# One soft-cap attention and soft mixture-of-experts kernel: two instead of three of every seven chunks share their exponential with VectorE, and the dispatch transposes and sums stand earlier in the loop

## The chip, the cores and the metric

The kernel runs on one core of a Trainium2 chip. The metric is the device time of one launch in microseconds (us). The kernel before the change took 330.87 us, the median of three runs that lie between 330.65 and 331.65 us.

In a core, TensorE multiplies matrices (PE in the profile; PEld is its loading of weights), ScalarE evaluates functions such as tanh and exp (ACT), VectorE does elementwise work (DVE), GpSimd does casts, copies and issues DMAs (POOL), and SyncE issues DMAs (SP). Each engine takes its own instructions in the order in which the program gives them, and an instruction that waits for another engine holds up all that stand behind it.

## The reference, cut to what matters

```python
# q, k, v: (8 batches, 12 heads, 448 tokens, 64); cap = 30
scores = (q @ k.T) / sqrt(64)
scores = cap * tanh(scores / cap)
attn   = softmax(scores, axis=-1)
x      = (attn @ v) as (8 * 448, 768)

# soft mixture of experts: phi (768, 32), w1 (8, 768, 1024), w2 (8, 1024, 768)
logits = x @ phi
d = softmax(logits, axis=0)                  # over all 3584 tokens: into the 32 slots
slot_in = d.T @ x                            # 4 slots for each of the 8 experts
slot_out[e] = relu(slot_in[e] @ w1[e]) @ w2[e]
c = softmax(logits, axis=1)                  # over the 32 slots: back to the tokens
out = c @ slot_out
```

## The kernel before, in words

**Attention.** Twelve heads of a batch are three quads of four heads, so there are 24 quads, each of two pairs of heads. The scores of a pair are 7 tiles of 128 keys (64 of either head) by 448 queries. The 336 tiles of all pairs are cut into 56 chunks of 6, and the main loop runs over chunks, `for j in range(NCH)`. Seven chunks are one batch, so the loop's pattern repeats with a period of seven iterations, and an iteration is named below by its number or by j % 7. In iteration j

- ScalarE does tanh on the two halves of chunk j (line 291, three tiles each, from PSUM) and then exp on the whole of chunk j - 1 (line 295), in place in the buffer `ex`. The scores are capped, so no maximum is taken off;
- TensorE multiplies `ex` of an earlier pair with v (line 331, `pv`, in two passes that share one PSUM buffer), and makes the scores of both halves of chunk j + 1 (line 282, `sc`, two PSUM buffers);
- VectorE normalizes each pass (lines 341 and 342, `rec` and `xq`).

**Work between.** Everything else is put into this loop by hand: `at(j, slot, f, ...)` hangs a call into a slot of iteration j. Slot "0" is at the iteration's start, "a" follows the first pass of `pv`, "b" the first half of the next scores, "c" the second pass of `pv`, and "d" the second half of the next scores. What shares a slot runs in the order in which it was hung there. Among these calls are the transposes of k and q (line 250, `kps` and `qps`, copied out by VectorE at 252 as `kT` and `qT`), the casts of v by GpSimd (260 and 261), transposes of x and logits (357 and 368, `xps` and `lps`, taken out at 359 and 373), matmuls on a tile of ones without a use of their own (`spare`, 521, `junk`), and DMAs of the weights by GpSimd (109 and 113).

For batch b with j = 7b there are also `e_exp` (line 379: the exponentials `E` of the logits, repeated fourfold by GpSimd at 385 as `e`) in iteration j + 11, `e_norm` (392 `zps`: their sum over tokens, added to `zacc` at 396, or copied there at 394 for batch 0) in j + 13, `e_transp` (404 `eps`: four transposes, copied out as `ET` at 405) and, for every other batch, `e_sums` (414 `wps`, and a reciprocal `winv` at 415). The transposes `kps`, `qps`, `xps`, `eps` and the results `lps`, `zps`, `wps` all use one PSUM buffer, `psT`: what comes next on TensorE waits until the engine that reads the one before has done so.

**The shared exponentials.** For a chunk j in the list `shared`, ScalarE's exp leaves the first of the six tiles out (it is `128x2240` in place of `128x2688`), and VectorE computes that tile in three parts of seven instructions on 128x448 elements: part 0 makes the exponent and the mantissa from bits (lines 307, 309, 311), part 1 and part 2 evaluate a polynomial (313, 314, then 316, 317). In the kernel before, `shared` holds the chunks with j % 7 of 1, 3 and 5 from 8 on, 20 in all.

**After the loop** come the last pairs, the slots' sums, the two layers of the experts (weights loaded to the chip or, for part of the second layer, to DRAM and from there once attention's buffers are free), and the output tiles, which VectorE and ScalarE take out and SyncE stores.

Of the kernel before, what the change touches and what calls it, by code (L numbers as in the profile page):

```python
# [32 lines left out]
def kernel(  # L33
# [20 lines left out]
    cap = float(cap)  # L54
# [6 lines left out]
    NCH = NTILE // CH  # L61
# [237 lines left out]

    shared = [j for j in range(NCH - 2) if j % 7 in (1, 3, 5) and j > 7] if cap < 80 else []

    def poly_exp(j, part):
        t, bits = exs[j][:, 0, :], 2.0 ** 23
# [135 lines left out]
    def at(j, slot, f, *a):  # L441
        if j < 0:
            j, slot = 0, "b"
        aux.setdefault((j, slot), []).append((f, a))
# [8 lines left out]
    def quad_in(Q, cast_k, cast_q, k_in, q_in, v_in):  # L453
        if 0 < Q < NQ:
            for nm, when in (("k", cast_k), ("q", cast_q)):
                at(*when, *((cast, nm) if Q == 1 else (load, nm, Q + 1)))
            at(*k_in, transp, "k", Q)
            at(*q_in, transp, "q", Q)
            at(*v_in, vcast, Q)

    for b in range(B):
        j = b * PER
        if b == 0:
            quad_in(1, (0, "a"), (0, "b"), (0, "d"), (1, "a"), (2, "d"))
        else:
            quad_in(3 * b + 1, (j - 1, "b"), (j, "a"), (j - 1, "d"), (j, "c"), (j + 1, "d"))
        quad_in(3 * b + 2, (j, "d"), (j + 1, "c"), (j + 2, "b"), (j + 2, "d"),
                (j + 4, "d"))
        quad_in(3 * b + 3, (j + 4, "a"), (j + 5, "a"), (j + 3, "d"), (j + 5, "c"),
                (j + 6, "d"))  # L470
        p = 6 * b
        at(j + 1, "d", spare, 34 if b == 0 else 10)
        at(j + 2, "d" if b == 0 else "a", spare, 4 if b == 0 else 14)
        if b:
            at(j + 2, "c", spare, 8)
        at(j + 3, "d", spare, 10 if b == 0 else 4)
        at(j + 4, "a", x_transp, p)
        at(j + 5, "a", x_transp, p + 1)
        at(j + 6, "a", x_transp, p + 2)
        at(j + 5, "d", logits, 3 * b)  # L480
        if b < B - 1:
            at(j + 7, "a", x_transp, p + 3)
            at(j + 8, "a", x_transp, p + 4)
            at(j + 7, "d", logits, 3 * b + 1)
            at(j + 9, "a", x_transp, p + 5)
            at(j + 9, "d", logits, 3 * b + 2)
            at(j + 11, "0", e_exp, b)
            at(j + 11, "d", slot_sums, b)
            if b < B - 2:
                at(j + 15, "c", e_transp, b)  # L490
            if b < B - 2:
                at(j + 13, "d", e_norm, b)
            if b % 2:
                at(j + 15, "d", e_sums, b // 2)
    for j in shared:
        for part, (dj, slot) in enumerate(((0, "a"), (0, "c"), (1, "b" if j % 7 == 1 else "a"))
                                          if j % 7 < 5 else ((0, "c"), (1, "a"), (1, "c"))):
            at(j + dj, slot, poly_exp, j, part)
    for n, job in enumerate(wjobs):
        at(1 + n * (NCH - 5) // len(wjobs), "b", *job)  # L500
    for j, slot, n in ((0, "a", 10), (0, "c", 10), (1, "b", 10), (1, "c", 8)):
# [251 lines left out]
    for n in range(B // 2 * NT):  # L753
        bb, c = divmod(n, NT)
# [61 lines left out]
```

## Time and profile before, and how to read it

| | before |
|---|---|
| median of three runs | 330.87 us |
| the profiled execution | 330.65 us, of which the span from the first to the last instruction is 328.9 us |
| busy: PE, ACT, DVE, POOL | 279.5, 278.6, 214.9, 141.3 us |
| mean granted TensorE clock | 0.95 of full speed |
| exp by ACT (line 295) | 132.1 us in 58 instructions: 35 of 128x2688, 20 of 128x2240, and 3 smaller at the end |
| tanh by ACT (line 291) | 141.3 us in 113 instructions |
| DMA moved on average | 206 GB/s |

A row of a timeline gives the start in us, the duration in us, the engine, the line, the operation, what it writes and reads with shapes, and how often; in square brackets stands the idle time of the engine just before, with what ended it. A row of the waits gives who waited for whom, and then the time in total, how often, and the longest. A row of the stages gives the window, its length, each engine's busy time with the number of instructions in brackets (PE, PEld, DVE, ACT, POOL), the granted clock of TensorE, the mean busy share of the DMA engines (overlapping packets can bring it above 1) and GB/s.

Iterations are found in the trace by ScalarE's rows: two tanh and one exp are one iteration. Iteration 9 starts at 47.38 us, 16 at 82.29, 23 at 116.60, 30 at 152.02, 37 at 185.98, 44 at 220.12 and 51 at 254.40 us. Tanh of the last chunk is done before 278.6 us.

### The profile page before, as it was taken

How to read it: one execution, taken by the hardware profiler on the slowest of the kernel's cores; microseconds unless marked ns; L12 is line 12 of the kernel's file. 1: busy time of each engine (PE TensorE's matmuls, PEld its weight loads, DVE VectorE, ACT ScalarE, POOL GpSimd, SP SyncE). 2: the span in 40 equal slices, each digit the busy share in tenths (PEclk: the TensorE clock that was granted, in tenths of full speed). 3: DMA queues.
4: the chain of work that ended last, by engine and by line, in shares of the span. 5: the costliest groups of instructions: out<-in, count | busy, mean ns of one | idle time of the engine just before them, and what ended most of it. 6: DMA issues, size and time to landing. Idle time of an engine off the chain costs nothing.

```text
span 328.9 us, 9405 instructions
## 1 busy us (share of the span) xinstructions
PE 279.5 (85%) x4071; PEld 195.9 (60%) x4071; DVE 214.9 (65%) x521; ACT 278.6 (85%) x208; POOL 141.3 (43%) x178
## 2 busy tenths in 40 slices
PE   8899989979997979979897899799979898998710
PEld 6667666656665656756575567576656667753300
DVE  3624577775788578767876767877786674427830
ACT  4999999996999799979998999989997999326720
POOL 4584660852566452575367516643761230000000
PEclk9999999987999799979997999999988999999975
DMA  7999999899799999999799997999899428977996
GB/s 258 205 198 180 223 189 220 158 180 226 137 156 190 232 168 155 163 196 195 126 184 221 176 189 129 185 230 205 141 205 195 107 96 259 343 267 290 390 411 250
DMA packets 57481, 67.64 MB, mean 206 GB/s; under 512 B 3808, under 2 KB 53600, under 8 KB 57440
## 3 DMA queue, kind: packets, MB, share of 16 engines
q0 software_dynamic: 42448, 35.31, 70.3%
q1 hardware_dynamic: 14704, 31.50, 27.7%
q8 instruction: 32, 0.52, 0.6%
q10 hardware_dynamic: 288, 0.23, 0.2%
q14 instruction: 9, 0.07, 0.1%
HBM read 91.32 MB, written 18.87 MB: 335 GB/s over the span
## 4 chain that ended last, share of the span: by engine, by line
PE 40%; DVE 33%; ACT 18%; DMA 3%; issue 2%; DVEq 0%; ACTq 0%
PE pv L331 14%; ACT ex L291 9%; ACT ex L295 8%; PE sc L282 7%; DVE xq L342 6%; DVE xp L314 3%; DVE ex L317 3%; PE junk L521 3%; PE xps L357 3%; PE kps L250 3%; DVE xp L316 2%; DVE xp L313 2%; DVE xm L309 2%; DVE rec L341 2%; DMA out_dram<-ob 2%; DVE xe L311 2%
## 5 line engine op out<-in xcount | busy, mean ns | idle before, releaser
L291 ACT ACTIVATE ex<-sc 128x1344 bf16<-128x1344 f32 (+1 forms) x113 | 141.3, 1317 | 15.0 <-PE pv L331 7.7
L295 ACT ACTIVATE ex<-ex 128x2688 bf16<-128x2688 bf16 (+4 forms) x58 | 132.1, 2282 | 0.1
L331 PEld LDWEIGHTS <-ex 128*128 128x128 bf16 x1344 | 81.7, 100 | 24.5 <-DVE xq L342 11.4
L331 PE MATMUL pv<-vbd,ex 128*128 128x130 bf16 x1274 | 93.2, 226 | 2.3 <-DVE xq L342 0.8
L282 PE MATMUL sc<-qT,kT 64*64 64x448 bf16 x672 | 80.1, 367 | 1.7 <-ACT ex L291 1.5
L260 POOL CAST vbd<-vraw 64x896 bf16<-64x896 f32 x23 | 23.1, 1006 | 69.5 <-PE pv L331 50.6
L341 DVE RECIPROCAL rec<-pv 128x4 f32<-128x4 f32 x91 | 16.5, 181 | 38.8 <-PE pv L331 38.8
L342 DVE TENSOR_TENSOR xq<-pv,rec 128x256 bf16<-128x256 f32 x91 | 38.6, 425 | 3.1
L385 POOL COPY e<-E 128x512 bf16<-128x512 bf16 x9 | 7.2, 795 | 77.4 <-issue 36.7
L282 PEld LDWEIGHTS <-kT 64*64 64x64 bf16 x672 | 25.6, 106 | 19.9 <-issue 2.6
L521 PEld LDWEIGHTS <-ones 128*128 128x128 bf16 x428 | 26.0, 101 | 7.8 <-DVE xq L342 3.1
L521 PE MATMUL junk<-ones 128*128 128x128 bf16 x391 | 29.1, 219 | 1.5 <-DVE xq L342 1.0
L261 POOL CAST vbd<-vraw 64x896 bf16<-64x896 f32 x23 | 26.4, 1149 | 1.2
L252 DVE COPY kT<-kps 128x896 bf16<-128x896 bf16 x23 | 14.3, 622 | 19.3 <-PE kps L250 19.2
L250 PE MATMUL kps<-ident,kb 128*64 128x128 bf16 x308 | 14.2, 236 | 12.2 <-DVE zacc L396 9.8
L109 POOL DMA_DIRECT2D w1b<-in_moe_w_dram x32 | 24.4, 765 | 0.0
L357 PE MATMUL xps<-ident,xq 128*128 128x128 bf16 x188 | 19.3, 228 | 5.8 <-DVE winv L415 2.4
L172 POOL DMA_DIRECT2D qb<-in_q_dram x22 | 16.1, 734 | 15.5 <-PE qps L250 9.1
L250 PEld LDWEIGHTS <-kb 128*64 128x64 bf16 x308 | 11.3, 118 | 17.8 <-issue 17.7
L359 DVE COPY xT<-xps 128x512 bf16<-128x512 bf16 x47 | 19.6, 417 | 2.4 <-PE xps L357 2.4
L357 PEld LDWEIGHTS <-xq 128*128 128x128 bf16 x188 | 14.1, 102 | 7.7 <-issue 7.7
L314 DVE SCALAR_TENSOR_TENSOR xp<-xp,xm 128x448 f32<-128x448 f32 x20 | 17.8, 890 | 0.7
(117 smaller groups left out, 309.3 us busy)
## 6 DMA issues: line engine op xcount, KB each, us to landing
w1b<-in_moe_w_dram POOLq DMA_DIRECT2D x32, 384.0 KB, 8.5
vraw<-in_v_dram SPq DMA_DIRECT2D x23, 448.0 KB, 4.0
w2d<-in_moe_w_dram POOLq DMA_DIRECT2D x20, 384.0 KB, 8.4
w2t<-w2d SPq DMA_DIRECT2D x20, 384.0 KB, 5.3
out_dram<-ob SPq DMA_DIRECT2D x8, 768.0 KB, 8.7
qb<-in_q_dram POOLq DMA_DIRECT2D x22, 224.0 KB, 6.5
kb<-in_k_dram POOLq DMA_DIRECT2D x22, 224.0 KB, 7.7
w2b<-in_moe_w_dram POOLq DMA_DIRECT2D x12, 384.0 KB, 8.2
```

What stands on the lines that cost most here:

```text
L109: pool.dma_start(out=w1b[e][:, js, fs], in_=w1r[:, e, js, fs])
L250: pe.transpose(ps[h * HP:h * HP + HP, c, :], src[:, h, c * DH:(c + 1) * DH], ident)
L260: pool.tensor_copy(t[0:HP, :, :, 0:DH], raw[0:HP])
L261: pool.tensor_copy(t[HP:P, :, :, DH + 1:VW - 1], raw[HP:P])
L282: pe.matmul(sc[cs, u, 0:S], qkT["k", Q][r, c, cs], qkT["q", Q][r, :, cs], start=True, stop=True)
L291: act.activation(exs[j][:, half * CS + u0:half * CS + u1, :], sc[:, u0:u1, 0:S], ACT.Tanh, scale=qk_scale / cap)
L295: act.activation(exs[j][:, u0:u1, :], exs[j][:, u0:u1, :], ACT.Exp, scale=cap)
L314: dve.scalar_tensor_tensor(xp, xp, POW2[2], xm, ALU.add, ALU.mult)
L331: pe.matmul(pvs[pr, half][:, n, 0:VW], exs[j][:, u, GOFF[g]:GOFF[g] + P], vbds[Q % 2][:, h, c, :], start=(c == 0 and n == 0), stop=(c == N ...
L342: dve.tensor_tensor(xq[Q][:, 2 * half:2 * half + 2, h * P:(h + 1) * P] .rearrange("p g (i d) -> p g i d", i=2), pv[:, :, :, 0:DH], rec.to_ ...
L357: pe.transpose(ps[:, g, :], xq[Q][:, g, h * P:(h + 1) * P], ident)
L521: pe.matmul(junk if home is None else home, ones, ones, start=True, stop=True)
```

## The change

Three edits. The chunks with j % 7 of 5 leave `shared`: 14 of the 20 stay, and ScalarE does the whole exp of chunks 12, 19, 26, 33, 40 and 47. `e_transp` moves from slot "c" of iteration j + 15 to slot "d" of j + 12 (from j % 7 = 1 to 5), where it stands ahead of the logits. `e_sums` moves from slot "d" of j + 15 to slot "d" of j + 14 (from j % 7 = 1 to 0), also ahead of the logits there. The parts of the exponentials that stay keep their slots; the third hunk only writes them more shortly. Buffers, loads and everything after the loop are the same.

```diff
-    shared = [j for j in range(NCH - 2) if j % 7 in (1, 3, 5) and j > 7] if cap < 80 else []
+    shared = [j for j in range(NCH - 2) if j % 7 in (1, 3) and j > 7] if cap < 80 else []
...
             if b < B - 2:
-                at(j + 15, "c", e_transp, b)
+                at(j + 12, "d", e_transp, b)
             if b < B - 2:
                 at(j + 13, "d", e_norm, b)
             if b % 2:
-                at(j + 15, "d", e_sums, b // 2)
+                at(j + 14, "d", e_sums, b // 2)
     for j in shared:
-        for part, (dj, slot) in enumerate(((0, "a"), (0, "c"), (1, "b" if j % 7 == 1 else "a"))
-                                          if j % 7 < 5 else ((0, "c"), (1, "a"), (1, "c"))):
-            at(j + dj, slot, poly_exp, j, part)
+        for slot, part in (("a", 0), ("c", 1)):
+            at(j, slot, poly_exp, j, part)
+        at(j + 1, "b" if j % 7 == 1 else "a", poly_exp, j, 2)
```

## The prediction

> **What bounds the kernel now.** I read the page's busy times first, then who ScalarE waits for, then who TensorE waits for, then one place of the timeline, and last the stages.
>
> ```profile
> PE 279.5 (85%) x4071; PEld 195.9 (60%) x4071; DVE 214.9 (65%) x521; ACT 278.6 (85%) x208; POOL 141.3 (43%) x178
> ...
> PEclk9999999987999799979997999999988999999975
> ```
>
> TensorE and ScalarE are equally busy, VectorE is far behind, and the clock row has dips that come back. ScalarE finishes attention near 281 us, so until then it hardly rests. Its waits between 47 and 255 us, the six periods that the change touches:
>
> ```profile
> ACT ex L291 <- PE pv L331: 7.7, 6, 1.7
> ACT ex L291 <- PE sc L282: 5.1, 8, 1.2
> ```
>
> These 12.8 us are all it waits there: tanh stands until TensorE delivers scores. In the timeline every wait above 1 us is at the first or second tanh of an iteration with j % 7 = 1 (15, 22, 29, ...), so TensorE is late once a period. For whom it waits itself, in the same window:
>
> ```profile
> PE kps L250 <- DVE zacc L396: 9.8, 5, 2.0
> ...
> PE xps L357 <- DVE winv L415: 2.1, 2, 1.0
> PE kps L250 <- DVE zacc L394: 2.0, 1, 2.0
> ```
>
> Six times, once a period, TensorE stands 2 us ahead of `kps`, because `zps` of `e_norm` holds `psT` until VectorE has taken it into `zacc`. What VectorE does meanwhile, in iteration 20:
>
> ```profile
> 104.94 0.88 DVE L316 SCALAR_TENSOR_TENSOR xp<-xp,xm 128x448 f32<-128x448 f32 x1
> ...
> 105.85 1.25 DVE L317 SCALAR_TENSOR_TENSOR ex<-xp,xe 128x448 bf16<-128x448 f32 x1
> ...
> 107.03 0.15 DVE L396 TENSOR_TENSOR zacc<-zps,zacc 128x1 f32<-128x1 f32 x1
> ...
> 107.23 0.58 PE L250 MATMUL kps<-ident,kb 128*64 128x128 bf16 x14 [2.02 <-DVE zacc L396]
> ...
> 110.08 1.70 PE L331 MATMUL pv<-vbd,ex 128*128 128x130 bf16 x14
> 110.73 1.29 ACT L291 ACTIVATE ex<-sc 128x1344 bf16<-128x1344 f32 x1 [1.10 <-PE pv L331]
> ```
>
> Lines 316 and 317 are part 2 of the exponential of chunk 19, one with j % 7 = 5: the very part that the change removes stands ahead of `zacc` and makes the wait. Soon after, `pv` takes 1.70 us where the undisturbed pass takes 0.98, and ScalarE's gap opens. The stages show why, beside two undisturbed ones:
>
> ```profile
> 12.15:47.38 35.23, 32.64 (x478) 23.16 (x477) 17.16 (x50) 35.20 (x25) 24.18 (x29) 1.00 1.11 190
> 82.29:104.75 22.46, 20.79 (x324) 14.74 (x320) 18.40 (x45) 22.46 (x18) 12.54 (x16) 1.00 0.91 158
> 108.00:112.00 4.00, 4.00 (x45) 2.90 (x44) 1.59 (x5) 2.90 (x2) 1.58 (x3) 0.57 1.20 262
> ```
>
> Behind the wait the granted clock is 0.57. In iterations 2 to 9 and 16 to 20 ScalarE is busy all the time at a clock of 1.00. So ScalarE bounds most of a period, and VectorE's queue, through TensorE, some 2.5 us of it.
>
> **ScalarE's new work.** The rows from which its pace without gaps follows:
>
> ```profile
> 84.63 2.08 ACT L295 ACTIVATE ex<-ex 128x2240 bf16<-128x2240 bf16 x1
> 86.59 2.48 ACT L291 ACTIVATE ex<-sc 128x1344 bf16<-128x1344 f32 x2
> 88.93 2.47 ACT L295 ACTIVATE ex<-ex 128x2688 bf16<-128x2688 bf16 x1
> 91.27 0.34 ACT L379 ACTIVATE E<-lg 128x128 bf16<-128x128 f32 x1
> ```
>
> From start to start the short exp takes 86.59 - 84.63 = 1.96 us, two tanh 2.34, the full exp 2.34. Six exps grow by 2.34 - 1.96 = 0.38 us: 2.3 us on the engine that bounds.
>
> A rule speaks against the change here: the Trainium skill, Perfetto Trace Analysis, Identifying the Most-Contended Engine, names the engine of highest occupancy as the one to relieve. Going by that alone (ScalarE at 85%, VectorE at 65%) the time would be 330.65 + 2.3 = 332.9 us. The waits above say that the share of VectorE hides a place where it comes last, and I go by them.
>
> **ScalarE's pace without gaps.** Iterations 16 to 20 took 22.46 us. The two others of a period (j % 7 of 0 and 1) have two tanh and a full exp, 4.68 us each. That makes 31.82 us a period now and 31.82 + 0.38 = 32.20 after. From iteration 9 (47.38 us) to 51 (254.40) six periods took 207.02 us, 34.50 each; the 2.68 us lost in each are the waits and the slower restart behind them. If no gap is left, a period falls by 34.50 - 32.20 = 2.30 us, six by 13.8.
>
> **Does TensorE follow?** VectorE loses six times 396 + 409 + 394 + 625 + 890 + 682 + 813 = 4.21 us, 25 us in all; none of it counts but what stands ahead of a waiting TensorE. The period from 185.98 to 220.12 us kept the full clock; TensorE was busy 29.42 of its 34.14 us. Of its 4.72 us idle:
> - the wait for `zacc` falls from 2.02 us to about 0.45, which is what `wps` waits for `ET` when VectorE is free: -1.57;
> - `e_sums` in its old place waited 0.45 for `ET` and then 1.03 for `winv` behind line 314 (1.26 us there). In the new one `ET` is long there, and `logits` waits for `winv` without a polynomial ahead: -1.48 + 0.45. Every other period has this;
> - `e_transp` now stands ahead of `logits`, which use the same `psT`, so `lps` waits for the copy of line 405 (0.38 us): +0.45, by the same row. Bounds: 0, if `qT` and the copy are through early, and 0.88, the weight load's wait for `ET` in the old place. Part 0 of the polynomial no longer stands there, so I take the middle. In `e` no wait is hidden: GpSimd has it ready within 1 us of `E`, some 8 us before slot "d" of iteration j + 12.
>
> TensorE then needs 34.14 - 1.57 - 1.48 + 0.45 + 0.45 = 31.99 us a period. That is below ScalarE's 32.20, but by only 0.2. So I charge 0.35 us a period for tanh that still waits a little (the smallest waits of today are 0.43 to 0.48): 2.1 us in all, with bounds of 0 and 6.
>
> **The clock.** Five half-clock stretches (by the length of the matmul rows, from about 72, 109, 143, 177 and 245 us on) begin at the end of such a wait or within 2 us; the sixth wait, near 211 us, had none. I take them as its consequence and let them go with it. The Trainium skill, TensorE: Matmul & The Clock Gate, HAM oscillation — how this bites in real kernels, would have only gaps of above some 3.4 us slow the clock. By it 2.02 us are too short, the dips have another cause and stay; the price of that is the first rival's.
>
> **The other pieces.** Behind 254.40 us, the wait of 0.46 us at iteration 52 and the 0.2 us before it go too (`e_sums` of batch 5 has left iteration 50): -0.6. What is after the loop is the same and starts earlier. DMA: the loads stand in their slots, so they come 6% faster; iterations 2 to 9 ran at 4.7 us each, as after, with a busy share of 1.11 and no wait for a load, so I cost it at nothing.
>
> **Sum.** 330.65 - 13.8 + 2.1 - 0.6 = 318.35 us for an execution like the profiled one. The median of the runs is 0.22 above it: 318.6 us.
>
> **The rivals.**
> - The clock still dips once a period, from the idle time that is left in slots "d". In iteration 48 the stretch lengthened `kps` by 0.38 us, `pv` by 0.72, `xps` by 0.25: 1.35 us. TensorE then needs 31.99 + 1.35 = 33.34 us a period and sets the pace: 1.14 us above ScalarE's, times six and with the residue kept, 318.6 + 6.8 = 325.4. For it: the dips come from little. Against it: the undisturbed stages with waits of 0.3 to 0.5 have none.
> - Slower: the waiting point only moves. `psT` now goes from `qps` over `eps`, `lps`, `xps` to `zps` and `kps` in two iterations, each with a VectorE read in between. If these waits and a dip that follows keep tanh waiting as long as today, ScalarE's 2.3 us come on top: 332.9 us. It decides from 2.68 - 0.38 = 2.3 us lost per period. For it: six uses of one buffer in a row. Against it: no other VectorE work is queued there but the norms.
> - DMA sets the pace: shares near 1 in most stages, time as before, 330.9. Against it: neither TensorE nor ScalarE waits for a load in these stages.
>
> **How the numbers follow.** Forecast 0.68 (315.2 to 321), dips stay 0.12 (321 to 329), no change by DMA 0.03, slower 0.17. The low end has no residue and one half-clock stretch less behind the loop, where the clock is 0.87 on average: 318.6 - 2.1 - 1.35 = 315.2. The range 315.2 to 329 leaves out the last two cases. About 0.3% is what a measurement of this kernel tells from no change; by that faster has 0.80, the same 0.03, slower 0.17.
>
> **What would show it.** Right: `kps` waits under 0.6 us for `zacc`, no half clock before 250 us, exp 2.3 us longer in sum, tanh waiting under 3 us between iterations 9 and 51, a period near 32.5 us. Wrong: `lps` or `xps` waiting 1 us or more in iterations with j % 7 of 5 or 6, dips in other places, or tanh waiting for `sc` in most iterations, which would say that TensorE is the bound.

## The result and the profile after

The changed kernel takes 315.32 us (median of four runs, 315.19 to 315.44), the kernel before 331.25 us in the median of its four. The ratio is 0.952 with a 95% interval of 0.9502 to 0.9539. The profiled execution took 315.40 us with a span of 313.6 us, 15.25 us less than the one before. All ratios leave out executions more than 1.5% longer than the shortest of the same kernel; the medians keep them. On the chips of the experiments the kernel before took 326 to 331 us, so a ratio there says more than a time.

From the page of the changed kernel: busy times, granted clock, and the chain of waits by engine.

```profile
PE 272.0 (87%) x4071; PEld 190.6 (61%) x4071; DVE 191.5 (61%) x479; ACT 278.3 (89%) x208; POOL 137.6 (44%) x178
...
PEclk9999999999999999999999999999999999999975
...
ACT 69%; PE 17%; DVE 4%; DMA 3%; issue 2%; DVEq 0%; ACTq 0%
```

ScalarE is as busy as before in a shorter span, and the clock dips only at the end. The chain before was

```profile
PE 40%; DVE 33%; ACT 18%; DMA 3%; issue 2%; DVEq 0%; ACTq 0%
```

Now ScalarE carries 69% of the span. The waits of TensorE over the whole execution:

```profile
PE sc L282 <- ACT ex L291: 4.4, 12, 0.5
...
PE lps L368 <- DVE ET L405: 2.9, 6, 0.5
...
PE kps L250 <- DVE zacc L396: 1.2, 5, 0.2
...
PE lps L368 <- DVE winv L415: 0.9, 3, 0.3
```

The wait for `zacc` fell from 2 us each to 0.25, and TensorE now waits for ScalarE twelve times. Iteration 20 again, from the timeline:

```profile
101.89 0.25 PE L392 MATMUL zps<-ones,e 128*128 128x1 bf16 x4
...
102.18 0.16 DVE L396 TENSOR_TENSOR zacc<-zps,zacc 128x1 f32<-128x1 f32 x1 [0.23 <-PE zps L392]
...
102.39 0.58 PE L250 MATMUL kps<-ident,kb 128*64 128x128 bf16 x14 [0.25 <-DVE zacc L396]
```

VectorE itself is idle ahead of `zacc` now. Last the stage of the six periods, which begins at 47.23 and ends at 240.23 us:

```profile
47.23:240.23 193.00, 176.00 (x2723) 125.85 (x2719) 130.25 (x338) 193.00 (x134) 102.63 (x128) 1.00 1.12 195
```

ScalarE works in all of the 193.00 us, at a TensorE clock of 1.00: 32.17 us a period, where it was 34.50. So the difference of the spans is 14.02 us in the six periods (207.02 - 193.00), 1.13 behind them (74.50 - 73.37) and 0.15 ahead of them, 15.3 in all.

### The profile page after: what moved, and what is told of

Read it like the earlier page. It is cut to its first block, busy times and chain, and to the rows that moved or that the text cites. A ratio compares the mean times of both kernels' runs of the same rounds, so it can differ in the third digit from the quotient of the medians.

```text
span 313.6 us, 9357 instructions
## 1 busy us (share of the span) xinstructions
PE 272.0 (87%) x4071; PEld 190.6 (61%) x4071; DVE 191.5 (61%) x479; ACT 278.3 (89%) x208; POOL 137.6 (44%) x178
## 4 chain that ended last, share of the span: by engine, by line
ACT 69%; PE 17%; DVE 4%; DMA 3%; issue 2%; DVEq 0%; ACTq 0%
ACT ex L291 36%; ACT ex L295 32%; PE pv L331 4%; DMA out_dram<-ob 2%; PE sc L282 2%; PE so_ps L689 2%; PE hp L662 2%; PE junk L521 2%; DMA kraw<-in_k_dram 1%; DVE xq L342 1%; PE op L767 1%; PE op L723 1%; ACT ob L776 1%; DVE obh L725 1%; PE xps L357 1%
## 5 line engine op out<-in xcount | busy, mean ns | idle before, releaser
L291 ACT ACTIVATE ex<-sc 128x1344 bf16<-128x1344 f32 (+1 forms) x113 | 163.7, 1721 | 0.8 <-PE sc L282 0.8
L295 ACT ACTIVATE ex<-ex 128x2688 bf16<-128x2688 bf16 (+4 forms) x58 | 158.1, 2754 | 0.1
L331 PEld LDWEIGHTS <-ex 128*128 128x128 bf16 x1344 | 77.9, 97 | 23.7 <-DVE xq L342 13.7
L331 PE MATMUL pv<-vbd,ex 128*128 128x130 bf16 x1274 | 89.2, 220 | 2.5 <-DVE xq L342 0.8
L282 PE MATMUL sc<-qT,kT 64*64 64x448 bf16 x672 | 78.6, 358 | 5.1 <-ACT ex L291 4.4
L260 POOL CAST vbd<-vraw 64x896 bf16<-64x896 f32 x23 | 22.5, 978 | 64.8 <-PE pv L331 56.1
L261 POOL CAST vbd<-vraw 64x896 bf16<-64x896 f32 x23 | 23.9, 1041 | 1.2
L252 DVE COPY qT<-qps 128x896 bf16<-128x896 bf16 x23 | 14.2, 618 | 5.5 <-PE qps L250 5.5
L250 PE MATMUL qps<-ident,qb 128*64 128x128 bf16 x308 | 12.8, 222 | 4.1 <-DVE lg L373 4.0
L172 POOL DMA_DIRECT2D kb<-in_k_dram x22 | 16.0, 728 | 0.0
L113 POOL DMA_DIRECT2D w2d<-in_moe_w_dram x20 | 15.1, 761 | 0.0
```

The costliest lines, as they stand in the source:

```text
L172: (sp if nm == "v" else pool).dma_start(out=t, in_=quad_ap(nm, Q))
L252: dve.tensor_copy(t, ps)
L260: pool.tensor_copy(t[0:HP, :, :, 0:DH], raw[0:HP])
L261: pool.tensor_copy(t[HP:P, :, :, DH + 1:VW - 1], raw[HP:P])
L282: pe.matmul(sc[cs, u, 0:S], qkT["k", Q][r, c, cs], qkT["q", Q][r, :, cs], start=True, stop=True)
L291: act.activation(exs[j][:, half * CS + u0:half * CS + u1, :], sc[:, u0:u1, 0:S], ACT.Tanh, scale=qk_scale / cap)
```

## The experiments

Two questions were open: whether the wait for `zacc` with the half clock behind it is the whole story, and whether VectorE's load or the place of its work makes the wait.

**The exponentials alone.** The changed kernel with the two moves undone.

```diff
-                at(j + 12, "d", e_transp, b)
+                at(j + 15, "c", e_transp, b)
-                at(j + 14, "d", e_sums, b // 2)
+                at(j + 15, "d", e_sums, b // 2)
```

> Only the third exponential goes; e_transp and e_sums keep their old slots. Theory (part 2 of the third exponential ahead of zacc is what made TensorE and then tanh late): tanh has no gap at j % 7 = 1, a period of ScalarE is 32.2 us, and the time 315 to 317.5 us; the old waits of TensorE for ET and winv stay, 0.45 and up to 1 us every other period, and may show as three tanh waits of 0.5 us. Rival (the two moves carry a good part of the gain): 319 to 326 us, with tanh waits left at j % 7 of 1 to 3.

316.10 us, ratio 0.965 (0.960 to 0.970). ScalarE waits for nothing between 40 and 265 us. Its six periods, from 47.20 to 240.95 us, take 193.75 us, against 193.00 in the changed kernel. The third exponential carries nearly the whole gain; the moves add some 0.7 us in these two executions.

**The moves alone.** The kernel before with both moves, and its three exponentials.

```diff
-                at(j + 15, "c", e_transp, b)
+                at(j + 12, "d", e_transp, b)
-                at(j + 15, "d", e_sums, b // 2)
+                at(j + 14, "d", e_sums, b // 2)
```

> Only e_transp and e_sums move; the third exponential stays with its parts where they were. Theory: kps still waits 2 us for zacc once a period behind lines 316 and 317, the clock still dips, lps waits in addition for ET behind part 0: 328 to 333 us. Rival (the moves matter most): 318 to 325 us.

330.2 us, ratio 1.006 (1.002 to 1.010): no gain. TensorE's waits between 40 and 265 us, and the clock:

```profile
PE kps L250 <- DVE zacc L396: 11.0, 5, 2.2
PE lps L368 <- DVE ET L405: 7.0, 6, 1.3
...
PE kps L250 <- DVE zacc L394: 2.0, 1, 2.0
```

```profile
PEclk9999999977999999999999999999999999999975
```

The wait for `zacc` stays, and `lps` waits 1.2 us each for `ET` behind part 0 of the polynomial. The move of `e_transp` is good only where no polynomial stands in slots "c" and "d". The clock did not do what was expected: it dips once, from about 67 to 77 us, beginning behind the `lps` wait of 1.31 us, and from 78.5 to 262 us it is 1.00 although `kps` waits 2.2 us for `zacc` five times there. Even so the later five periods (counted from one exp of line 379 to the next) take 33.95 to 34.49 us. So TensorE's waits make tanh late without any half clock, and a wait of 2.2 us alone does not bring the half clock.

**The wait by itself.** Scratch work on VectorE at the place where part 2 was, with ScalarE's work as in the changed kernel.

```diff
+    def dve_extra(n):
+        for _ in range(n):
+            dve.scalar_tensor_tensor(xp, xp, POW2[2], xm, ALU.add, ALU.mult)
+
+    for b in range(B - 2):
+        at(7 * b + 13, "c", dve_extra, 3)
```

> The changed kernel with three more VectorE instructions of line 316's form on scratch tiles in slot c of iteration j + 13, once a period, so that they stand between zps and zacc as part 2 did (1.9 to 2.5 us); they feed nothing. ScalarE's work is that of the changed kernel. Theory (this wait and the half clock behind it make the whole difference): kps waits some 2 us for zacc again, the clock dips again, 324 to 331 us. Rival (VectorE's total load or the third exponential's other parts matter): under 320 us.

336.27 us, ratio 1.026 (1.023 to 1.030), above the range that was expected. The waits of TensorE between 45 and 262 us, and the clock:

```profile
PE kps L250 <- DVE zacc L396: 13.4, 5, 2.7
...
PE kps L250 <- DVE zacc L394: 2.7, 1, 2.7
```

```profile
PEclk9999999998999899969997999789997999999975
```

The wait came out at 2.7 us and not 2.0, and the clock dips again. Six such waits cost 336.27 - 315.36 = 20.9 us, 3.5 us each. With no other edit, this one wait brings back more than the change had won. VectorE's load by itself is not what does it: by the page it is busy 207.6 us here, less than the 214.9 of the kernel before, and the kernel is slower.

**TensorE kept busy in the wait.** The kernel before, with 26 matmuls on ones between `zps` and `kps`.

```diff
                 at(j + 13, "d", e_norm, b)
+                at(j + 13, "d", spare, 26)
```

> The kernel before with 26 matmuls on ones (spare, some 1.5 us) put between zps and kps, where TensorE waited 2 us for zacc. The wait for VectorE stays, only TensorE is busy meanwhile. Theory (the half clock is a consequence of that idle time): no half clock before 250 us, tanh still late by some 0.9 us a period at j % 7 = 1 and 0.7 us every other period; by the difference of the five disturbed periods to the undisturbed one (2.2 against 0.9 us of idle time, 1.3 us each) 330.7 - 6.4 = 324 us, between 321 and 327. Rival (the dips have another cause, and gaps below 3.4 us do not slow the clock): dips stay, 330 to 332 us.

324.86 us in the profiled execution, 321.86 in a second one, ratio 0.987 (0.978 to 0.996) by these two. Its clock row and ScalarE's waits between 40 and 265 us:

```profile
PEclk9999999999999999999999999999999999999995
```

```profile
ACT ex L291 <- PE sc L282: 4.0, 9, 0.5
ACT ex L291 <- PE pv L331: 1.5, 5, 0.4
```

In this execution the dips are gone with the idle time, although VectorE still makes `kps` wait until the same work is done. Tanh waits 5.5 us, where it waits 13.3 in the same window of the kernel before. Two more executions took 327.81 and 328.70 us at a mean granted clock of 0.96, where these two have 0.98 to 0.99; without a trace of them it stays open whether the matmuls always end the dips.

The six periods, from iteration 9 at 49.84 us to iteration 51 at 248.90, take 199.06 us in place of 207.02. So 7.96 us went with the half clock, 1.6 us for each of the five stretches. (The whole time is only 5.8 us shorter because here the first tanh wait 3.0 us for scores, not 0.8, and iteration 9 starts 2.46 us later.) The kernel before, on this chip, points the same way without an edit: at a mean granted clock of 0.950 it took 330.56 to 330.88 us, at 0.965 or 0.966 326.11 to 326.65. The other 6.06 of the 14.02 us are TensorE's time in the wait, with the 0.7 us of the moves, less what ScalarE's new work costs.

**The third exponential in other slots.** The changed kernel with 20 shared chunks, the parts of j % 7 = 5 in slots a and c of j and a of j + 1.

```diff
-    shared = [j for j in range(NCH - 2) if j % 7 in (1, 3) and j > 7] if cap < 80 else []
+    shared = [j for j in range(NCH - 2) if j % 7 in (1, 3, 5) and j > 7] if cap < 80 else []
```

> The changed kernel with the third exponential put back (20 chunks shared), but its parts in slots a and c of iteration j and a of j + 1, as the parts of j % 7 = 3 have them, so that nothing of it stands between zps and zacc. Theory (place, not amount of VectorE work): ScalarE's period falls from 32.17 to 31.79 us without gaps, 315.3 - 2.3 = 313.0 us, or up to 315.5 if lps, which now waits for ET behind lines 313 and 314 (1.3 us), makes tanh late in some periods. Rival (VectorE has no room for a third exponential in any place): 319 to 331 us, with a half clock once a period.

327.56 us, ratio 0.998 (0.994 to 1.002): the gain is gone, and my theory missed. The profiled execution was one of the longer ones, 330.28 us; those of the ratio have 324.80 to 328.63 us at a clock of 0.949 to 0.959. TensorE's waits in it between 40 and 265 us:

```profile
PE lps L368 <- DVE ET L405: 6.7, 6, 1.1
...
PE eps L404 <- DVE qT L252: 3.9, 4, 1.2
...
PE kps L250 <- DVE zacc L396: 1.2, 5, 0.2
```

`zacc` is quick, but now `eps` and `lps` stand for VectorE behind parts 0 and 1, at the very place to which `e_transp` was moved. The clock halves in this kernel too (0.50 from 201 to 208 us). The first two periods, though, take 31.80 and 31.79 us without a wait of ScalarE, as the theory said; the loss begins in the third.

**Nothing that reads `psT` behind a polynomial.** Three exponentials, part 2 earlier, `e_transp` earlier, `e_norm` and `e_sums` in j + 14.

```diff
-                at(j + 15, "c", e_transp, b)
+                at(j + 12, "b", e_transp, b)
-                at(j + 13, "d", e_norm, b)
+                at(j + 14, "d", e_norm, b)
-                at(j + 15, "d", e_sums, b // 2)
+                at(j + 14, "d", e_sums, b // 2)
-                                          if j % 7 < 5 else ((0, "c"), (1, "a"), (1, "c"))):
+                                          if j % 7 < 5 else ((0, "c"), (1, "a"), (1, "b"))):
```

> Three exponentials a period as in the kernel before, but nothing that reads psT stands behind a polynomial: part 2 of j % 7 = 5 in slot b of j + 1, e_transp in slot b of j + 12, e_norm and e_sums in slot d of j + 14. Theory (only the place counts): ScalarE runs without gaps at 31.79 us a period, 315.3 - 6 x 0.38 = 313.0 us, up to 315 if some tanh still wait. Rival (with the third exponential TensorE, which has under 1 us a period to spare, always falls behind): 318 to 330 us, with tanh waiting for scores in most periods.

333.9 us, ratio 1.016 (1.012 to 1.021), slower than before. One place of its timeline (VectorE, then GpSimd):

```profile
103.75 1.38 DVE L316 SCALAR_TENSOR_TENSOR xp<-xp,xm 128x448 f32<-128x448 f32 x1
105.17 1.25 DVE L317 SCALAR_TENSOR_TENSOR ex<-xp,xe 128x448 bf16<-128x448 f32 x1
106.35 0.17 DVE L341 RECIPROCAL rec<-pv 128x4 f32<-128x4 f32 x1
```

```profile
103.73 0.92 POOL L260 CAST vbd<-vraw 64x896 bf16<-64x896 f32 x1 [3.37 <-PE pv L331]
104.70 1.25 POOL L261 CAST vbd<-vraw 64x896 bf16<-64x896 f32 x1
```

Part 2 stands ahead of the normalization of `pv`, and at the time of GpSimd's casts of v each of its instructions takes twice its 0.62 us. The next `pv` waits 2.3 us for `xq`: the wait has moved to the other PSUM buffer.

**`e_norm` later.** The kernel before with this move alone.

```diff
-                at(j + 13, "d", e_norm, b)
+                at(j + 14, "d", e_norm, b)
```

> The kernel before with e_norm alone moved from slot d of j + 13 to slot d of j + 14. The wait of kps for zacc goes; kT is now copied behind part 2, so xps behind it waits some 1 us for kT, and the waits of e_sums stay. Theory: the wait shrinks from 2 to about 1 us, half clocks become rare: 318 to 325 us. Rival (the wait only changes its name, kps or xps wait 2 us for kT): 327 to 331 us.

324.07 us in the profiled execution, ratio 0.986 (0.980 to 0.991), within the range of the theory. What waits, though, was not foreseen: not `xps` for `kT` but `pv` for line 317, which writes the tile that this `pv` reads, 7.5 us in six times. One half-clock stretch is left (0.51 from 180 to 190.5 us).

**The third exponential clear of the casts.** As the run in other slots, but with `e_transp` in slot "a" of j + 12, ahead of part 0.

```diff
-    shared = [j for j in range(NCH - 2) if j % 7 in (1, 3) and j > 7] if cap < 80 else []
+    shared = [j for j in range(NCH - 2) if j % 7 in (1, 3, 5) and j > 7] if cap < 80 else []
-                at(j + 12, "d", e_transp, b)
+                at(j + 12, "a", e_transp, b)
```

> The changed kernel with the third exponential back in slots a, c and a of j + 1, and e_transp in slot a of iteration j + 12, ahead of the polynomial's part 0 there. So no copy out of psT but lg stands behind a polynomial, and part 2 is over before GpSimd casts v in that iteration. Theory A (the place of each part decides, not the load): no gap at ScalarE, 31.79 us a period, 313.0 us, up to 315 with a few waits left. Theory B (with 31.8 us a period TensorE, which had some 0.6 us a period to spare at 32.17, and its waits for VectorE are the bound): tanh waits for scores in every period, once late the clock halves, 320 to 330 us.

317.94 us, ratio 0.970 (0.966 to 0.975), between the two theories. The clock stays full in the loop, and ScalarE waits 1.6 us in all. Yet six periods take 194.94 us (iteration 9 at 47.05, 51 at 241.99), 32.49 each, not 31.79. TensorE's waits between 45 and 262 us:

```profile
PE xps L357 <- DVE ET L405: 4.8, 6, 0.8
...
PE lps L368 <- DVE qT L252: 2.9, 6, 0.8
```

Twice a period TensorE stands 0.5 to 0.8 us for readers of `psT` behind the polynomial's parts. By its own pace ScalarE would need 6 x 31.79 = 190.7 us; 4.2 us are lost again, 1.8 of them idle time and the rest mostly in tanh pairs that take 2.47 to 2.68 us from start to start in place of 2.34. That is more than the 2.3 us taken off it. The loss builds up: from one exp of line 379 to the next the first two periods take 31.80 and 31.81 us, the other four 32.5 to 33.3. What wears out in the first two is not shown.

**Fewer matmuls on ones,** in that kernel and in the changed one.

```diff
-        at(j + 1, "d", spare, 34 if b == 0 else 10)
-        at(j + 2, "d" if b == 0 else "a", spare, 4 if b == 0 else 14)
+        at(j + 1, "d", spare, 34 if b == 0 else 6)
+        at(j + 2, "d" if b == 0 else "a", spare, 4 if b == 0 else 8)
```

> The kernel of the run beside it, with two of the groups of matmuls on ones cut from 10 to 6 and from 14 to 8 in each period: some 0.6 us less for TensorE. Theory A: as that run, 313 to 315 us. Theory B: TensorE catches up where it could not before, clearly faster than the run beside it, 313 to 320 us.

> The changed kernel with the same cut of its matmuls on ones. ScalarE is the bound there, so under both theories 315.3 us, unless the cut itself makes the clock halve, which would show as 317 us or more.

With the third exponential 316.49 us, ratio 0.964 (0.961 to 0.968): 1.5 us better, but with the same 194.9 us in the six periods and the same two waits of TensorE (4.8 and 2.9 us). In the changed kernel 315.31 us, ratio 0.960 (0.954 to 0.966): two runs took 313.9 and 314.1 us, another 316.6 and the profiled one 319.32, so whether the cut gains anything stays open. In the profiled one the clock did halve, from about 51.4 to 63 us (0.56 on average). That began behind a wait of 1.06 us of TensorE for ScalarE, with no `zacc` wait near; tanh then waited 2.15 us, and that period took 34.48 us, the other five 32.17.

The changed kernel took 315.36 us once more beside the others:

> The changed kernel beside the others on the same chip: 315.3 us, with no gap of ScalarE between iterations 9 and 51.

It has two levels, 315.1 to 315.4 and 318.0 us. In its profiled execution at the upper one ScalarE has no gap in the six periods either, but iteration 9 starts at 49.88 us and not at 47.23: the first tanh wait 3.0 us for scores, where the lower level has 0.8. No version with the third exponential had a lower median than this kernel.

## Why the prediction was right

- **The place of the wait** was right: part 2 ahead of `zacc`, TensorE, then tanh. Taking the exponential away gave nearly all the gain, and putting other VectorE work there took more than that back.
- **The sizes at TensorE** held: `kps` waits 0.25 us for `zacc` (0.45 said), `lps` 0.48 for `ET` (0.45) and 0.30 for `winv` (0.45).
- **ScalarE's pace** without gaps: 32.17 us against 32.20, from rows of the profile before.
- **The residue** was the mis-sized term. I charged 0.35 us a period, 2.1 in all, since TensorE's need of 31.99 us lay only 0.2 below ScalarE's pace. It was 0.0. I take the need to have been too high: it counted all other idle time of TensorE as needed, and in the six periods after the change TensorE waits 3.7 us for ScalarE, 0.6 us a period. Without this term the sum is 316.25 us; the profiled execution took 315.40.
- **Behind the periods** the gain was 1.13 us where 0.6 was said, and 0.15 us came ahead of them. The wait of 0.46 us at iteration 52 was sized too low: from the exp of iteration 51 to that of 52 it is 5.16 us before and 4.30 after, 0.86 less, and the restart behind line 379 there gives 0.21 more.
- **The low end of the range**, 0.1 us below the result, holds in part by luck. It counted one half-clock stretch less behind the loop, 1.35 us, and there nothing changed: from the last exps to the end it is 50.35 us before and 50.30 after. The gains that I had not counted, 0.2 us in the periods, 0.5 behind and 0.15 ahead of them, happened to stay below 1.35.
- **The clock** went with the wait in the changed kernel, and matmuls in the gap ended the dips in the profiled execution. The Trainium skill, TensorE: Matmul & The Clock Gate, HAM oscillation — how this bites in real kernels, warns of idle gaps above 3.4 us; here half-clock stretches followed waits of 2.0 us in five of six cases. But my step from the wait to the dip was too simple: with the moves alone five waits of 2.2 us kept the full clock, and with fewer matmuls on ones a stretch began behind a wait of 1.06 us. What else decides stays open.
- **The rule of the busiest engine** would have said 332.9 us. The work moved to ScalarE is in its 32.17 us a period, and the wait that it ended on the engine that looked idle was worth several times as much.
- **The rival of the moved wait** was real, but for another kernel: with a polynomial in those slots `eps` and `lps` wait and the clock halves. **The rival of DMA** was not: its busy share rose from 1.06 to 1.12 in the six periods, and neither TensorE nor ScalarE waits for a load there.

## What to carry to other kernels

An engine that is busy 65% of the time can still set the pace, if a short operation of it that holds a shared buffer is queued behind long ones. Look for a wait that comes back once a period, find what stands ahead of its releaser in that engine's queue, and price the work there by the wait, not by the busy share. Moving the long work helps only if its new place has no short reader behind it either: the three other places tried here all gave the wait a new name, at 0.970 to 1.016 of the time before, and none beat taking the work away.

## What the runs showed of the hardware that was not expected

- VectorE beside GpSimd: lines 316 and 317, with two tensors as inputs, take 0.62 us alone and 1.25 to 1.38 while GpSimd casts v. The Trainium skill, SBUF — State Buffer, SBUF: two separate sides, has a port pair of the two engines that one holds while the other waits; the rows fit that.
- In an unbroken stretch ScalarE's recorded durations grow, though its pace does not: two tanh show 2.58 us at 47 us and 3.24 at 212 us, from start to start 2.34 in both. After a gap they are short again: one tanh shows 1.29 us in the profile before. The pace is read from starts; the mean of line 291 on the page rose from 1317 to 1721 ns with no tanh slower. For the same reason line 295's sum rose from 132.1 to 158.1 us, so the sign "exp 2.3 us longer in sum" can't be read from the page.
